# Padded Q/K projection weights in place of scatter DMAs, in a gated mix of infini-attention and a token-mixing MLP

## The chip, the cores and the metric

The kernel runs on one core of one Trainium2 chip. The metric is the device time of one execution in microseconds (us). An execution is called fast or slow by its time (slow is more than 1.5% above the fastest of the same kernel).

Engine names: PE is TensorE (matmul), PEld its weight loads, DVE VectorE, ACT ScalarE, POOL GpSimd, SP SyncE. L474 is line 474 of the kernel's file.

## The reference

The input x has 2048 rows of 640. One branch is attention with a compressive memory: 32 heads of 20 columns, four segments of 512 rows, causal softmax within a segment and a memory M, z carried from segment to segment. The other is an MLP that mixes along the rows. A gate mixes the two.

```python
g = sigmoid((x * gate_w).sum(-1, keepdims=True))
# branch a, for each segment s of 4:
p = softmax(qs @ ks.T * 20**-0.5 + causal_mask)
o = sig(beta) * (phi(qs) @ M) / (phi(qs) @ z + 1e-6) + (1 - sig(beta)) * (p @ vs)
M = M + phi(ks).T @ vs ;  z = z + phi(ks).sum(rows)
a = concat(o) @ wo
# branch b:
u = gelu(layernorm(x).T @ w1 + b1)      # 640 x 1536
b = (u @ w2 + b2).T                     # 2048 x 640
out = g * a + (1 - g) * b
```

## The kernel before

The 32 heads stand in eight groups of four. In the layout of a group (qA for Q, kA for K) each head has 32 of the 128 partitions: row 0 is a spare row (the "safe" variant puts the row maximum there; its partner in kA is -1), rows 1 to 20 are the head, the rest are zeros. The projection matmul makes 128 plain columns at a time, so 20-row heads lie across them, and small DMAs carry each head to its rows:

```python
def proj_T(s, which, dq):                   # dq = 0..4: 128 plain columns of wq or wk
    st = pl["stg"].tile([P, L], BF, ...)
    pq = p1([P, 512], name="pT" + which)
    for c in range(DC):                     # 5 matmuls of 512 columns
        nc.tensor.matmul(pq[:, 0:L], lhsT=w_sb[:, c, dq * P:(dq + 1) * P], rhs=xT[:, c, s * L:(s + 1) * L], ...)
    evac(st[:], pq[:, 0:L])
    for h in range(H):                      # every head that ends in these columns
        ...
        nc.sync.dma_start(out=dst[row:row + DH, g, :], in_=st[e0 - dq * P:e1 - dq * P, :])
```

The main loop runs over segments and groups. Beside a group's scores and exponentials it does the projections of the next segment (in groups 0 to 4 only), the previous group's product with V, and a part of the MLP's second half:

```python
for s in range(NSEG):
    for g in range(G):
        st_exp(s, g)                        # scores psB (32-row matmuls, one per head), exp on ScalarE, mask on GpSimd
        if prev is not None: pv_post(*prev) # pacc = P @ V, 21 columns for each head
        ...
        if g < TPS: nat_v(s + 1, g); nat_k(s + 1, g)
        ...
        if g < DC: proj_T(s + 1, "q", g); proj_T(s + 1, "k", g)
        if g % 2 == 0: tail_y(s * TPS + j)  # 24 matmuls of the MLP, result scaled into yb by ScalarE
        elif s >= 1:   tail_b(s - 1, j, ...) # output projection, store of one row tile through GpSimd
```

Ahead of it stands the prologue: transposes of x, segment 0's projections, layer-norm statistics, and the first MLP matmul (w1, six loads of 1 MB through three buffers).

## Time and profile before

| | before |
|---|---|
| time, median of the first 4 runs | 461.99 us (460.63 to 465.0) |
| span of the profiled run | 461.5 us, clock 0.86 |
| prologue, to the first exponential | 137.8 us |
| segments 0 to 3 | 81.3, 85.2, 78.1, 57.4 us |
| end, after the last exponential | 21.7 us |

The prediction below shows the table of stages. Two lines of the page give the whole at a glance: engine busy time, and the granted TensorE clock in 40 equal slices, in tenths of full speed.

```profile
PE 384.5 (83%) x3636; PEld 217.9 (47%) x3636; DVE 191.0 (41%) x469; ACT 251.7 (55%) x413; POOL 104.9 (23%) x174
...
PEclk9755989997997999956599998599989889877877
```

TensorE is busy 83% of the span, but the clock dips again and again below 9. The 30 clock records of this trace have only two values, 1.0 and 0.5; a 7 is a mixture. The profiled run took 463.31 us, 0.3% above the median.

```profile
L489 PE MATMUL pacc<-vs,PT 128*128 128x21 bf16 x116 | 4.6, 179 | 0.9 <-POOL PT L476 0.9
L471 PE MATMUL psB<-qA,kA 32*128 32x512 bf16 x12 | 2.6, 599 | 0.0
```

These are the groups without projections. TensorE looks 82 to 92% busy and yet gets a clock of 0.62 and 0.73. Its work there is in part scores of only 32 rows (32*128) and products of only 21 columns; the largest single group in the window, 24 full-height matmuls of the MLP, has 7.7 us.

### The profile page before, as it was taken

To read this page: it belongs to the slowest core of one execution; us is meant where nothing else is said; L and a number is where in the kernel's file an instruction comes from. 1 tells how busy PE (TensorE), PEld (TensorE's weight loads), DVE (VectorE), ACT (ScalarE), POOL (GpSimd) and SP (SyncE) were. 2 spreads that over 40 slices of the span, in tenths; PEclk is the share of its full clock that TensorE was granted. 3 is DMA by queue.
4 is the path that set the end of the run, shared out by engine and by line. 5 is a ranking of instruction groups with operands and counts; after the bars stand their busy time and mean duration, and the time that the engine had idled before them with its cause. 6 is when DMAs were issued, how large, how long until landed. Compare 5 with 4: busy or idle time off the path is not lost.

```text
span 461.5 us, 9298 instructions
## 1 busy us (share of the span) xinstructions
PE 384.5 (83%) x3636; PEld 217.9 (47%) x3636; DVE 191.0 (41%) x469; ACT 251.7 (55%) x413; POOL 104.9 (23%) x174
## 2 busy tenths in 40 slices
PE   3604969967989998878999998999979799999971
PEld 3501437744754555534355554445535445445451
DVE  7178145000003466540457585254645533332342
ACT  2933724210234768566566647575545778777810
POOL 3000000000012223124222322342323244433321
PEclk9755989997997999956599998599989889877877
DMA  7970011129003013102001310021131120000001
GB/s 257 330 201 0 23 25 25 25 51 243 1 19 124 20 27 93 25 19 70 3 22 38 91 38 24 20 84 26 40 89 39 26 78 22 16 16 15 3 31 48
DMA packets 27817, 27.06 MB, mean 59 GB/s; under 512 B 3700, under 2 KB 25716, under 8 KB 27764
## 3 DMA queue, kind: packets, MB, share of 16 engines
q1 hardware_dynamic: 25122, 17.45, 13.7%
q0 software_dynamic: 2432, 8.91, 5.9%
q8 instruction: 30, 0.49, 0.5%
q14 instruction: 23, 0.19, 0.1%
q10 hardware_dynamic: 210, 0.02, 0.0%
HBM read 18.50 MB, written 2.62 MB: 46 GB/s over the span
## 4 chain that ended last, share of the span: by engine, by line
PE 52%; ACT 12%; SPq 10%; DMA 9%; DVE 8%; issue 6%; POOL 2%; ACTq 0%; DVEq 0%; POOLq 0%
PE py L518 14%; PE psB L471 9%; ACT PT L474 8%; SPq L199 8%; PE pu L363 7%; PE pTq L189 4%; PE pTk L189 4%; PE pv L144 4%; PE pk L155 4%; DMA qA<-stg_q 3%; DMA wq_sb<-in_A_wq_dram 3%; PE pacc L489 3%; DVE stats L287 3%; PE po L546 2%; POOL PT L476 2%
## 5 line engine op out<-in xcount | busy, mean ns | idle before, releaser
L474 ACT ACTIVATE PT<-psB 128x1024 bf16<-128x1024 f32 (+3 forms) x256 | 167.2, 711 | 41.7 <-PE psB L471 35.4
L476 POOL TENSOR_SCALAR_AFFINE_SELECT PT<-PT 128x512 bf16<-128x512 bf16 x128 | 83.5, 653 | 174.4 <-ACT PT L474 171.8
L471 PE MATMUL psB<-qA,kA 32*128 32x256 bf16 (+3 forms) x512 | 75.2, 331 | 10.3 <-ACT PT L474 9.0
L518 PE MATMUL py<-uT,w2c 128*128 128x320 bf16 x384 | 76.4, 342 | 0.6 <-DVE aseg L432 0.6
L363 PE MATMUL pu<-xs,w1c 128*128 128x320 bf16 x384 | 54.1, 304 | 7.5 <-DMA w1c<-in_B_w_dram 7.5
L471 PEld LDWEIGHTS <-kA 32*128 32x128 bf16 x512 | 24.7, 92 | 67.5 <-issue 61.0
L518 PEld LDWEIGHTS <-w2c 128*128 128x128 bf16 x384 | 37.4, 106 | 25.0 <-issue 6.2
L363 PEld LDWEIGHTS <-w1c 128*128 128x128 bf16 x384 | 37.9, 99 | 23.1 <-DMA w1c<-in_B_w_dram 7.9
L489 PE MATMUL pacc<-vs,PT 128*128 128x21 bf16 x1280 | 44.9, 174 | 2.4 <-POOL PT L476 2.3
L489 PEld LDWEIGHTS <-PT 128*128 128x128 bf16 x1280 | 38.4, 97 | 15.5 <-issue 9.8
L508 POOL DMA_DIRECT2D w2c<-in_B_w_dram x8 | 8.5, 1062 | 149.7 <-PE pu L363 129.9
L522 ACT ACTIVATE yb<-py,omgb,omg 128x320 bf16<-128x320 f32 x32 | 18.0, 613 | 39.7 <-PE py L518 39.7
L395 DVE CAST vs<-pv 128x320 bf16<-128x320 f32 x24 | 10.9, 489 | 67.4 <-PE pv L144 67.4
L366 ACT ACTIVATE uT<-pu,b1t 128x320 bf16<-128x320 f32 x24 | 11.3, 523 | 49.6 <-PE pu L363 49.6
L144 PE MATMUL pv<-wv_sb,xT 128*128 128x320 bf16 x160 | 32.7, 310 | 5.1 <-ACT stg_q L343 3.0
L546 PE MATMUL po<-wo_sb,aT 128*128 128x320 bf16 x160 | 32.2, 327 | 2.2 <-DVE at L501 1.5
L189 PE MATMUL pTq<-xT,wq_sb 128*128 128x512 bf16 x100 | 30.8, 429 | 2.4 <-DVE phikb L135 1.8
L492 DVE RECIPROCAL rr<-pacc 128x16 f32<-128x16 f32 x32 | 8.2, 256 | 50.1 <-PE pacc L489 49.3
L189 PE MATMUL pTk<-xT,wk_sb 128*128 128x512 bf16 x100 | 28.5, 419 | 0.4 <-DVE phikb L135 0.4
L133 DVE TENSOR_SCALAR e_q<-qA 128x512 bf16<-128x512 bf16 x24 | 8.7, 363 | 41.0 <-DMA qA<-stg_q 40.9
L155 PE MATMUL pk<-wk_sb,xT 128*128 128x320 bf16 x120 | 24.4, 334 | 0.0
L395 DVE COPY aT<-pta 128x640 bf16<-128x640 bf16 x16 | 7.7, 488 | 39.5 <-PE pta L532 39.5
(103 smaller groups left out, 368.6 us busy)
## 6 DMA issues: line engine op xcount, KB each, us to landing
w1c<-in_B_w_dram SPq DMA_DIRECT2D x6, 1024.0 KB
w2c<-in_B_w_dram POOLq DMA_DIRECT2D x8, 768.0 KB, 5.7
xs<-in_A_x_dram SPq DMA_DIRECT2D x4, 640.0 KB
out_dram<-osb POOLq DMA_DIRECT2D x16, 160.0 KB, 2.2
kA<-stg_k SPq DMA_DIRECT2D x112, 20.0 KB
qA<-stg_q SPq DMA_DIRECT2D x112, 20.0 KB
wv_sb<-in_A_wv_dram SPq DMA_DIRECT2D x1, 800.0 KB
wk_sb<-in_A_wk_dram SPq DMA_DIRECT2D x1, 800.0 KB
```

Source lines behind the costliest of these rows:

```text
L144: nc.tensor.matmul(pv[hh][:, 0:HALF], lhsT=xT[:, c, t * P:(t + 1) * P], rhs=wv_sb[:, c, hh * HALF:(hh + 1) * HALF], start=(c == 0), stop=( ...
L155: nc.tensor.matmul(pk[hh][:, 0:HALF], lhsT=xT[:, c, t * P:(t + 1) * P], rhs=wk_sb[:, c, hh * HALF:(hh + 1) * HALF], start=(c == 0), stop=( ...
L189: nc.tensor.matmul(pq[:, 0:L], lhsT=w_sb[:, c, dq * P:(dq + 1) * P], rhs=xT[:, c, s * L:(s + 1) * L], start=(c == 0), stop=(c == DC - 1))
L199: nc.sync.dma_start(out=dst[row:row + DH, g, :], in_=st[e0 - dq * P:e1 - dq * P, :])
L363: nc.tensor.matmul(pu[hh][:, 0:HALF], lhsT=w1c[:, t, f2 * P:(f2 + 1) * P], rhs=hs[:, t, hh * HALF:(hh + 1) * HALF], start=(t == 0), stop=( ...
L395: nc.vector.tensor_copy(out=out_view, in_=ps_view)
L471: nc.tensor.matmul(psB[:, rr, 0:Nq], lhsT=kA[32 * r:32 * r + 32, g, jt * P:(jt + 1) * P], rhs=qA[32 * r:32 * r + 32, g, jt * P:L], start=T ...
L474: nc.scalar.activation(out=pt[:, hp * NRT:(hp + 1) * NRT, :], in_=psB[:, :, 0:Nq], func=ACT.Exp, scale=SCALE)
L476: nc.gpsimd.affine_select(out=pt[:, :, 0:P], in_=pt[:, :, 0:P], compare_op=ALU.is_ge, fill=0.0, base=0, pattern=[[0, HG], [1, P]], channel ...
L489: nc.tensor.matmul(pacc[:, it, r, :], lhsT=PT[jt][:, r, (it - jt) * P:(it - jt + 1) * P], rhs=vs[:, jt, HG * g + r, :], start=(jt == 0), s ...
L518: nc.tensor.matmul(py[hh][:, 0:HALF], lhsT=w2c[:, ft, (t % 2) * P:(t % 2 + 1) * P], rhs=uT[:, ft, hh * HALF:(hh + 1) * HALF], start=(ft == ...
L546: nc.tensor.matmul(po[hh][:, 0:HALF], lhsT=aT[:, c, :], rhs=wo_sb[:, c, hh * HALF:(hh + 1) * HALF], start=(c == 0), stop=(c == DC - 1))
```

## The change

The intent: place the 20 columns of each head at the right places of zero-padded weights wq_pad, wk_pad of 8 x 128 columns, once. Then the projection of a group comes out in the group's layout, and the 288 scatter DMAs go. The price is 8 instead of 5 projections for Q and for K in each segment, on an engine that is already the bound. The diff brings more than its title says: a new order of the prologue (MLP before the projections of segment 0), projections spread over all eight groups, yb on VectorE, stores and w2 loads on SyncE.

```diff
+    wq_pad = persist.tile([P, DC, G * P], BF, name="wq_pad")
+    wk_pad = persist.tile([P, DC, G * P], BF, name="wk_pad")
 ...
+        nc.gpsimd.memset(wq_pad[:], 0.0)
+        nc.vector.tensor_copy(out=wq_pad[:].rearrange("p c (h w) -> p c h w", w=32)[:, :, :, 1:1 + DH],
+                              in_=wq_st[:].rearrange("p c (h d) -> p c h d", d=DH))
 ... (wk_pad likewise)
-    for i in range(2):
-        nc.vector.memset(qAb[i][:], 0.0)
-        nc.vector.memset(kAb[i][:], 0.0)
-        def proj_T(s, which, dq): ...            # with its scatters
+        def pg_q(s, g):
+            pq = p1([P, 512], name="pq")
+            for c in range(DC):
+                nc.tensor.matmul(pq[:, 0:L], lhsT=wq_pad[:, c, g * P:(g + 1) * P], rhs=xT[:, c, s * L:(s + 1) * L], ...)
+            evac(d["qA"][:, g, :], pq[:, 0:L])
+            ... (phi of it)
+        def pg_k(s, g): ...                      # likewise, kbias adds the -1 of the spare row
 ... (in the loop)
-                    if g < DC:
-                        proj_T(s + 1, "q", g)
-                        proj_T(s + 1, "k", g)
+                    pg_q(s + 1, g)
+                    pg_k(s + 1, g)
 ... (yb)
-                nc.scalar.activation(out=yb[...], in_=py[hh][:, 0:HALF], func=ACT.Identity, scale=omg[...], bias=omgb2[...])
+                if fast: nc.vector.tensor_scalar(out=yb[...], in0=py[hh][:, 0:HALF], scalar1=omg[...], scalar2=omgb2[...], ...)
 ... (queues)
-            nc.gpsimd.dma_start(out=w2c[:], ...)
+            nc.sync.dma_start(out=w2c[:], ...)
-            nc.gpsimd.dma_start(out=out[0, t * P:(t + 1) * P, :], in_=osb[:])
+            nc.sync.dma_start(out=out[0, t * P:(t + 1) * P, :], in_=osb[:])
 ... (prologue: statistics in two halves, MLP, transposes and gate, then segment 0's projections)
```

## The prediction

> **What bounds the kernel now.** I first read the list of cores: one core, 461.5 us, mean granted clock 0.86. Then I cut the span at the events that separate its stages (first projection matmul, first MLP matmul, last MLP matmul, first exp of each of the four attention segments, last exp) and asked for busy time per stage.
>
> ```profile
> core 0: us, PE busy (x) PEld busy (x) DVE busy (x) ACT busy (x) POOL busy (x), PEclk, DMA share, GB/s
> 0.00:41.40 41.40, 12.55 (x165) 10.71 (x166) 25.41 (x71) 18.87 (x29) 4.22 (x22) 0.72 0.73 219
> 41.40:74.90 33.50, 28.35 (x174) 16.00 (x173) 15.75 (x40) 19.67 (x31) 0.00 (x0) 0.89 0.09 20
> 74.90:134.80 59.90, 52.38 (x375) 36.94 (x373) 1.38 (x3) 10.39 (x22) 0.00 (x0) 0.94 0.26 64
> ...
> 137.80:219.10 81.30, 73.64 (x713) 37.79 (x713) 37.86 (x90) 53.00 (x90) 22.60 (x34) 0.83 0.19 55
> 219.10:304.30 85.20, 80.25 (x793) 43.15 (x792) 47.34 (x112) 52.72 (x89) 24.53 (x38) 0.86 0.14 41
> 304.30:382.40 78.10, 70.54 (x728) 37.59 (x726) 38.01 (x94) 48.91 (x80) 25.99 (x39) 0.93 0.16 47
> 382.40:439.80 57.40, 55.40 (x611) 28.59 (x610) 18.13 (x44) 45.92 (x72) 22.12 (x37) 0.85 0.04 13
> 439.80:461.50 21.70, 9.66 (x79) 6.18 (x78) 7.13 (x16) 0.01 (x1) 3.21 (x6) 0.69 0.11 42
> ```
>
> Prologue: 137.8 us to the first exp, of which the first 41.4 have almost no TensorE work. The first three segments (244.6 us) are TensorE-bound: it is busy 90 to 94%, at a clock of 0.83 to 0.93. The last has ScalarE at 80%. The groups of instructions give the unit costs.
>
> ```profile
> L474 ACT ACTIVATE PT<-psB 128x1024 bf16<-128x1024 f32 (+3 forms) x256 | 167.2, 711 | 41.7 <-PE psB L471 35.4
> L522 ACT ACTIVATE yb<-py,omgb,omg 128x320 bf16<-128x320 f32 x32 | 18.0, 613 | 39.7 <-PE py L518 39.7
> L189 PE MATMUL pTq<-xT,wq_sb 128*128 128x512 bf16 x100 | 30.8, 429 | 2.4 <-DVE phikb L135 1.8
> L189 PE MATMUL pTk<-xT,wk_sb 128*128 128x512 bf16 x100 | 28.5, 419 | 0.4 <-DVE phikb L135 0.4
> ```
>
> One group of four heads needs 8 exps, 8 x 711 ns = 5.7 us of ScalarE. The scatters show in the list of waits, beside the one stall of the MLP:
>
> ```profile
> DVE e_q L133 <- DMA qA<-stg_q: 40.9, 15, 6.2
> ACT yb L522 <- PE py L518: 39.7, 15, 6.3
> PE pu L363 <- DMA w1c<-in_B_w_dram: 7.5, 1, 7.5
> ```
>
> The 40.9 us are VectorE's, not the bound's; in the chain of waits that DMA has only 3% of the span (some 15 us). The 7.5 us are TensorE's: the w1 loads share SyncE's queue with the segment-0 scatters. In time order, this is how an even head group of segment 1 starts:
>
> ```profile
> 233.06 1.13 ACT L522 ACTIVATE yb<-py,omgb,omg 128x320 bf16<-128x320 f32 x2 [5.74 <-PE py L518]
> 233.37 0.40 PE L471 MATMUL psB<-qA,kA 32*128 32x512 bf16 x4
> ...
> 234.08 3.82 ACT L474 ACTIVATE PT<-psB 128x1024 bf16<-128x1024 f32 x5
> ```
>
> ScalarE stands idle 5.7 us while TensorE does projection and MLP work, then does yb, and only then the exps, whose input came during yb. And the prologue waits for the layernorm statistics, through the three transposes of the fast/safe test:
>
> ```profile
> 40.46 0.17 DVE L308 TENSOR_REDUCE gstat<-x 128x1 f32<-128x16 f32 x1
> 40.78 0.80 PE L318 MATMUL pg<-ident_f,gstat 128*1 128x128 f32 x3 [20.22 <-DVE gstat L308]
> 41.37 2.34 PE L189 MATMUL pTq<-xT,wq_sb 128*128 128x512 bf16 x5
> ```
>
> [...] at 47.63 and 48.71 us two groups of five 512-column projections start 1.08 us apart, 216 ns each[...]. [...] in 192.5 to 219.1 us, the light end of segment 0, TensorE is busy 21.8 of 26.6 us and the granted clock is 0.62. [...] The scatters go through SyncE[...]: they stand in the chain in pieces of 1.9 to 2.5 us, and issuing one costs SyncE 0.71. [...] no row of before is like the new padding copy.
>
> **The change, part by part.**
>
> *Projections.* 5 chunks of 128 columns become 8 padded groups: 3 more groups x 2 (q, k) x 5 matmuls = 30 more per segment, 30 x 0.216 = 6.5 us at full clock. The three segments that project ahead take +19.4; segment 0's also +6.5. Evictions: 16 instead of 10 per segment at 0.69 us on VectorE, +4.1 us, beside other work. Where the old loop projected only in head groups 0 to 4 and left 5 to 7 nearly empty, the new order has pq and pk in all eight; in groups 4 to 7 they lie between score matmuls, in ScalarE-limited time.
>
> *Scatters.* 288 small DMAs (144 each for q and k) go, with the waits of phi(q) on them and the block of w1 (7.5 us).
>
> *yb moves to VectorE* (in the diff, not in its title). In the last segment ScalarE sets the pace: from 376.15 to 388.87 us, two head groups, 12.72 us, it has 2 x 5.67 + 1.13 = 12.47 us of work. So 4 x 1.13 = 4.5 us go there; in segments 0 to 2 a little less than 0.6 us for each of 12 (exp input ready at about 233.6, exp at 234.1), some 6 us.
>
> *Prologue.* New order: statistics, MLP, transposes, gate, then segment-0 projections.
> - Statistics start with the first quarter of x, at 5.3 us, not at 26 (there behind 9 us of memsets and the gate). One row tile costs 0.86 us (28.18 to 29.04), 16 cost 13.8; with pieces between them 20.4. Then two padding copies stand before the last steps[...], then 1.9 us of small instructions: gstat at about 26, pg, first MLP matmul at 26.7.
> - 384 MLP matmuls at 136 ns = 52.4 (52.38 busy measured)[...]: 82.
> - 80 transposes evicted by two engines, 6 us; 80 gate matmuls 2.7; branch: 92.
> - V and K rows: 80 x 0.136 = 10.9, but VectorE needs 2.7 us per tile and four PSUM buffers recycle through ScalarE: 14. Memory update 2. Q and K 80 x 0.216 = 17.3. First exp at 126 to 127, against 137.8: **-11 us**. The statistics save 15, the stall 7.5; transposes and gate, no longer under the loads, give back 9[...].
>
> *Main loop.* [...] a head group lasts the exp-paced stretch (about 5.8 us before, 5.5 without yb) plus what the new order puts after the last score matmul. Counting matmuls there, in segment 1 before: 5.3, 3.9, 5.9, 5.0, 5.9, 0, 1.8, 0, sum 27.8; with 8 x 5.8 this makes 74.2 at full clock against 85.2 measured, a factor of 1.15. Segment 0 gives 71.9 against 81.3 (1.13), segment 2 66.4 against 78.1 (1.18). After, the same count gives 72.0, 78.8 and 72.8. With a factor of 1.10 (no DMA waits, fewer light stretches) they take 79.2, 86.7 and 80.1, together 246 against 244.6. The last segment: 57.4 - 4.5 = 52.9. Main loop 299 against 302: **-3**.
>
> *End.* Stores on SyncE instead of GpSimd, 0.55 us each of GpSimd time gone: -1 of 21.7.
>
> Sum: 461.5 - 11 - 3 - 1 = 446.5; I say 446.
>
> **The rivals.**
> 1. *The extra matmuls are paid in full.* If the factor stays at 1.15, the three segments take 257, +12.6 on 244.6: total about 457, the same within 2%. For it: TensorE already at 90 to 94%. Against: a part lies in exp-paced time.
> 2. *The evened load keeps the clock up.* The lost time of before is mostly in the light head groups (0.62, 0.73 and 0.84 at the ends of segments 0 to 2). If pq and pk hold the clock near 1 there, the factor falls to 1.04: 232.5, total about 432.
> 3. *VectorE becomes the bound.* It takes yb (some 0.49 us each) and the added evictions: segment 1 from 47.3 to about 55 us of 87. Not in sum[...]; bursts in head group 4 could add 1 us to each group: about 460.
> 4. *Prologue.* [...]
>
> **Range and chances.** Rivals 2 and 1 give 432 to 457; 4 us more for the prologue on the slow side, and 2 on the other: 430 to 461. The 2% line is at 452.7; my middle is 6.7 below it, and about two thirds of my range: faster 0.67, same 0.27, slower 0.06 (it would need rivals 1, 3 and 4 together).
>
> **What would show it.** First MLP matmul near 27 us, ending near 82, without a wait for w1; first exp near 127; segments near 79, 87, 80 and 53 us; ScalarE above 85% busy in the last; no scatter DMAs; granted clock in head groups 5 to 7 above 0.85. Wrong if the first MLP matmul comes after 33, if a segment exceeds 90 us, or if py or pq wait for VectorE by more than 10 us in all.

Three terms of its sums went: the time of the two padding copies ahead of gstat, a slow-clock term at the start of the MLP, and what rival 4 put on the prologue. With the cut terms the forecast came to 26.7 us for the first MLP matmul, 82 for the end of the MLP, -11 us for the prologue and 446.5 us in all; the terms that are left would give 23 and 75.4 us for the first two, and -13.5 us. The 216 ns are the distance between starts (109 of 122 such gaps at full clock in before are 215 or 216 ns); the 419 ns of the row are the mean length of a record, and these records overlap. The 2.7 us per tile on VectorE match three pairs of rows in the trace of before (0.95, 0.89 and 0.89 us). The 6 us for the evictions of the transposes are the author's estimate.

## More of the kernel before

The following answers are the busy times in groups 5 to 7 of segments 0 and 1 (columns: window and length, then PE, PEld, DVE, ACT, POOL busy with instruction counts, clock, DMA share, GB/s).

```profile
192.50:219.10 26.60, 21.82 (x212) 9.82 (x209) 6.68 (x21) 17.94 (x30) 8.51 (x13) 0.62 0.15 42
279.10:304.30 25.20, 23.12 (x240) 11.49 (x236) 10.75 (x29) 17.96 (x30) 8.98 (x14) 0.73 0.16 49
```

## The result

The kernel after takes 419.31 us (median of 10 runs, 418.39 to 420.61) against 461.99 (15 runs, 455.97 to 466.68). A ratio here is the mean time of one kernel's fast runs over the mean of the other's fast runs of the same rounds, with the profiled runs left out and "fast" judged among the rest, so it is not quite the ratio of the medians; it is 0.912, with a 95% interval of 0.909 to 0.915. The prediction of 446 (430 to 461) had the direction, but the result is 27 us below it and outside the range.

The answering two lines of the page of after:

```profile
PE 374.4 (90%) x3756; PEld 219.0 (53%) x3756; DVE 235.0 (56%) x542; ACT 226.4 (54%) x364; POOL 106.7 (26%) x162
...
PEclk9999999989999999998799999999999999999988
```

There are 120 more matmuls and 10 us less busy time. The clock is at 9 or more almost everywhere. The stages of after, cut at the same kinds of events (first MLP matmul, last MLP matmul, first exponential of each segment, last exponential; columns as above):

```profile
24.20:78.80 54.60, 54.60 (x389) 38.62 (x388) 1.93 (x10) 18.86 (x32) 0.00 (x0) 1.00 0.47 130
78.80:120.60 41.80, 38.88 (x358) 24.04 (x356) 30.53 (x57) 10.67 (x23) 8.21 (x4) 0.96 0.01 1
120.60:193.20 72.60, 70.54 (x724) 38.12 (x722) 46.54 (x100) 48.61 (x80) 23.42 (x33) 1.00 0.08 23
193.20:277.50 84.30, 81.36 (x839) 45.54 (x838) 56.95 (x129) 49.03 (x80) 21.61 (x34) 0.96 0.09 26
277.50:350.90 73.40, 71.08 (x762) 39.09 (x761) 49.02 (x109) 45.27 (x72) 20.91 (x33) 1.00 0.11 32
350.90:400.70 49.80, 48.45 (x627) 27.36 (x625) 23.98 (x56) 40.73 (x64) 19.83 (x31) 1.00 0.04 15
400.70:417.10 16.40, 8.92 (x78) 5.89 (x75) 7.14 (x16) 0.00 (x0) 0.64 (x1) 0.81 0.17 57
```

| stage | before | predicted | after | gain |
|---|---|---|---|---|
| prologue | 137.8 | 126.5 | 120.6 | 17.2 |
| segment 0 | 81.3 | 79.2 | 72.6 | 8.7 |
| segment 1 | 85.2 | 86.7 | 84.3 | 0.9 |
| segment 2 | 78.1 | 80.1 | 73.4 | 4.7 |
| segment 3 | 57.4 | 52.9 | 49.8 | 7.6 |
| end | 21.7 | 20.7 | 16.4 | 5.3 |
| sum | 461.5 | 446.1 | 417.1 | 44.4 |

The segments 0 to 2, which got 19.4 us more matmul work, became 14.3 us shorter. What the clock takes can be read from a table of stages: a stage of length t at mean clock c loses about (1 - c) t of TensorE time. Before, that is 0.17 x 81.3 + 0.14 x 85.2 + 0.07 x 78.1 = 31.2 us in segments 0 to 2, after it is 0.04 x 84.3 = 3.4 us. So 27.8 us come back, more than the padding costs. This is bookkeeping, as it counts idle time at half clock too. What the two tables show directly is that TensorE's idle time in these segments fell from 20.2 to 7.3 us, and its busy time by 1.45 us in spite of the added matmuls.

How the prologue starts in after, in order of time (start, us, engine, line, operation, bracket: what ended the idle time before it):

```profile
19.97 1.12 DVE L233 COPY wq_pad<-wq_st 128x3200 bf16<-128x3200 bf16 x1
...
23.50 0.17 DVE L191 TENSOR_REDUCE gstat<-x 128x1 f32<-128x16 f32 x1
...
23.81 0.58 PE L197 MATMUL pg<-ident_f,gstat 128*1 128x128 f32 x2 [17.04 <-DVE cmask L268]
```

The statistics are there at 23.50 us, against 40.46 before. The padding copy takes 1.12 us, less than the cut term of the prediction allowed.

The end, before and after (same columns):

```profile
454.64 1.01 DVE L550 SCALAR_TENSOR_TENSOR osb<-po,gt,yb 128x320 bf16<-128x320 f32 x2 [2.79 <-DMA out_dram<-osb]
455.95 0.54 POOL L553 DMA_DIRECT2D out_dram<-osb  x1 [3.26 <-DVE osb L550]
```

```profile
412.26 1.01 DVE L521 SCALAR_TENSOR_TENSOR osb<-po,gt,yb 128x320 bf16<-128x320 f32 x2 [0.52 <-PE po L517]
```

Before, the last output tile waits 2.79 us for an earlier store to give its buffer back, and 5.9 us lie between the end of that tile's work (455.65) and the end of the span (461.5). After, there is no such wait, and 3.8 us lie between (413.27 and 417.1).

### The profile page after: what moved, and what is told of

Read it like the earlier page. It is cut to its first block, busy times and chain, and to the rows that moved or that the text cites. A ratio compares the mean times of both kernels' runs of the same rounds, so it can differ in the third digit from the quotient of the medians.

```text
span 417.1 us, 9052 instructions
## 1 busy us (share of the span) xinstructions
PE 374.4 (90%) x3756; PEld 219.0 (53%) x3756; DVE 235.0 (56%) x542; ACT 226.4 (54%) x364; POOL 106.7 (26%) x162
## 3 DMA queue, kind: packets, MB, share of 16 engines
q1 hardware_dynamic: 31842, 21.11, 17.2%
## 4 chain that ended last, share of the span: by engine, by line
PE 79%; ACT 9%; DVE 4%; DMA 3%; SPq 2%; issue 2%; POOL 0%; ACTq 0%; POOLq 0%; DVEq 0%
PE psB L437 13%; PE py L484 13%; PE pu L222 13%; PE pq L367 9%; PE pk L394 9%; ACT PT L440 7%; PE pv L328 6%; PE po L517 5%; PE pk L339 4%; PE pacc L455 3%; DMA wk_sb<-in_A_wk_dram 2%; SPq L140 2%; PE pta L503 1%; ACT xT L246 1%; DMA xs<-in_A_x_dram 1%
## 5 line engine op out<-in xcount | busy, mean ns | idle before, releaser
L437 PE MATMUL psB<-qA,kA 32*128 32x256 bf16 (+3 forms) x512 | 68.4, 305 | 7.5 <-ACT PT L440 7.5
L484 PE MATMUL py<-uT,w2c 128*128 128x320 bf16 x384 | 60.1, 300 | 0.0
L437 PEld LDWEIGHTS <-kA 32*128 32x128 bf16 x512 | 24.5, 91 | 60.9 <-issue 54.9
L222 PE MATMUL pu<-hs,w1c 128*128 128x320 bf16 x384 | 54.6, 306 | 0.0
L394 PE MATMUL pk<-xT,wk_pad 128*128 128x512 bf16 x160 | 45.0, 381 | 0.0
L367 PE MATMUL pq<-xT,wq_pad 128*128 128x512 bf16 x160 | 44.6, 381 | 0.0
L484 PEld LDWEIGHTS <-w2c 128*128 128x128 bf16 x384 | 35.2, 98 | 15.8 <-issue 1.2
L489 DVE TENSOR_SCALAR yb<-py,omg,omgb 128x320 bf16<-128x320 f32 x32 | 18.1, 606 | 24.8 <-PE py L484 24.8
L397 DVE TENSOR_SCALAR kA<-pk,kbias 128x512 bf16<-128x512 f32 x32 | 24.0, 748 | 12.3 <-PE pk L394 10.2
L318 DVE CAST qA<-pq 128x512 bf16<-128x512 f32 x32 | 22.0, 688 | 11.5 <-PE pq L367 11.5
L517 PE MATMUL po<-wo_sb,aT 128*128 128x320 bf16 x160 | 27.9, 310 | 0.5 <-DVE aT L318 0.5
L313 ACT ACTIVATE e_q<-e_q 128x512 bf16<-128x512 bf16 x24 | 15.0, 626 | 20.6 <-DVE e_q L312 20.6
```

The source lines that it names most:

```text
L222: nc.tensor.matmul(pu[hh][:, 0:HALF], lhsT=w1c[:, t, f2 * P:(f2 + 1) * P], rhs=hs[:, t, hh * HALF:(hh + 1) * HALF], start=(t == 0), stop=( ...
L367: nc.tensor.matmul(pq[:, 0:L], lhsT=wq_pad[:, c, g * P:(g + 1) * P], rhs=xT[:, c, s * L:(s + 1) * L], start=(c == 0), stop=(c == DC - 1))
L394: nc.tensor.matmul(pk2[:, 0:L], lhsT=wk_pad[:, c, g * P:(g + 1) * P], rhs=xT[:, c, s * L:(s + 1) * L], start=(c == 0), stop=(c == DC - 1))
L397: nc.vector.tensor_scalar(out=d["kA"][:, g, :], in0=pk2[:, 0:L], scalar1=kbias[:, 0:1], scalar2=None, op0=ALU.add)
L437: nc.tensor.matmul(psB[:, rr, 0:Nq], lhsT=kA[32 * r:32 * r + 32, g, jt * P:(jt + 1) * P], rhs=qA[32 * r:32 * r + 32, g, jt * P:L], start=T ...
L484: nc.tensor.matmul(py[hh][:, 0:HALF], lhsT=w2c[:, ft, (t % 2) * P:(t % 2 + 1) * P], rhs=uT[:, ft, hh * HALF:(hh + 1) * HALF], start=(ft == ...
```

## The experiments

Twelve kernels were run; all gave correct results. Each batch of four shared one chip and its runs of before (medians 461.46, 460.40 and 462.62 us). Ratios of different batches that are less than about 1% apart are not told apart here. First comes the theory, then the runs by question. The theory after reading the traces was: the padding pays because it evens TensorE's load, and the clock follows the load. The main rivals were that yb on VectorE, the vanished scatter waits, the queues or the new prologue order did it.

**The padding alone (b_pad).** The kernel before with padded weights, one projection of Q and K in each of the eight groups and no scatters. The zeroing of qA and kA falls away with the scatters. Order of the prologue, yb and queues stay.

```diff
-        nc.vector.memset(qAb[i][:], 0.0)
-        nc.vector.memset(kAb[i][:], 0.0)
+    nc.vector.tensor_copy(out=w_pad[...][:, :, :, 1:1 + DH], in_=w_sb[...])      # for q and k
-                    if g < DC: proj_T(s + 1, "q", g); proj_T(s + 1, "k", g)      # 128 plain columns, then scatters
+                    proj_T(s + 1, "q", g); phi_q(s + 1, g); proj_T(s + 1, "k", g) # w_pad, straight into qA, kA
```

> The kernel before with the padded projections alone: padded weights built by two VectorE copies, eight groups spread over eight head groups, no scatters; the order of the prologue, the statistics, yb on ScalarE and the stores stay as before. Theory of the clock: segments 0 to 2 at a clock above 0.95 and 225 to 235 us together (244.6 before), prologue within 2 us of before (6.5 us more matmuls, 7.5 us less stall), total 443 to 452 us. Rival (most of the gain is the new prologue order and yb on VectorE): 456 to 465 us, clock below 0.92.

Measured: 424.56 us (421.56 to 427.75), ratio 0.9225 (0.912 to 0.933). That is most of the gain, and more than I expected (443 to 452 us): segments 0 to 2 came out as forecast, the prologue did not. The MLP and segment 3 of its stages, and the moment of the statistics:

```profile
61.60:115.20 53.60, 53.49 (x415) 38.39 (x411) 3.48 (x7) 12.67 (x26) 0.00 (x0) 1.00 0.22 60
...
346.10:402.30 56.20, 54.04 (x622) 28.75 (x619) 19.07 (x48) 45.68 (x72) 21.95 (x36) 0.88 0.04 13
```

```profile
30.57 0.17 DVE L304 TENSOR_REDUCE gstat<-x 128x1 f32<-128x16 f32 x1
```

The first exponential comes at 118.1 us, 19.7 earlier than before and even 2.5 earlier than in after, in the old order of the prologue. Two things go with it. VectorE no longer zeroes qA and kA (four memsets of 1.76 us), and its statistics begin at 5.28 us, no longer behind that and the gate; they are there at 30.57 instead of 40.46, and the first MLP matmul comes at 61.6 instead of 72.3. What the zeroing alone is worth and what the changed order of VectorE's work was not separated. And the MLP runs its 53.6 us without the stall for w1 (62.6 before), because no scatters stand in SyncE's queue ahead of the w1 loads. Segments 0 to 2 take 73.2, 81.0 and 73.8 us, all at clock 1.00. Segment 3 and the end (21.4 us) stay as before.

**yb on VectorE alone (b_yb_dve), and taken back from after (a_yb_act).** The edit of the first is the yb part of the diff above; the second is its reverse.

> The kernel before with yb on VectorE and nothing else changed. My prediction: 4.5 us off the last segment and some 6 off the others: 449 to 454 us, clock of segments 0 to 2 still 0.83 to 0.93. Rival (yb between the exps is what makes the light stretches and so the low clock): clock above 0.95, time below 440.

Measured: 461.31 us (452.81 to 464.21); three of four runs were slow, so there is no ratio. The one fast run, 452.81 us, lies within the expected 449 to 454, the median does not: this run decides nothing. The last segment of its profile (a slow run) takes 55.7 us.

> The kernel after with the scaling of the MLP output back on ScalarE in every segment. Theory: worth little in segments 0 to 2 where TensorE sets the pace (each within 1.5 us of after), but in the last segment, where the exponentials on ScalarE set the pace, it puts the eight 600 ns evictions back: last segment 55 to 58 us instead of 49.8 and a clock of 0.85 to 0.95 there; in all 424 to 428 us, 1.0% to 2.2% slower than after. Rival (ScalarE never binds; the last segment is shorter after for another reason, such as the stores): 418 to 421 us with the last segment at 49 to 51.

Measured: 421.58 us (419.29 to 421.84), ratio 0.919, which is 0.8% above the ratio of after, from another batch. The last segment takes 50.2 us at clock 1.00 with all eight evictions back on ScalarE. So yb was not what shortened segment 3. My expectation of 55 to 58 us was wrong, and so was the prediction's 4.5 us.

**Is it the load that keeps the clock? (b_fill)** To the kernel before I added ten useless matmuls of 512 columns and 128 rows in each of groups 5 to 7 of segments 0 to 2. That is 90 x 0.216 = 19.4 us of TensorE time that computes nothing used.

```diff
+                    else:                                   # groups 5 to 7
+                        pd = p1([P, 512], name="pfill")
+                        for c in range(2 * DC):
+                            nc.tensor.matmul(pd[:, 0:L], lhsT=wo_sb[:, c % DC, 0:P], rhs=xT[:, c % DC, 0:L], ...)
```

> The kernel before, plus ten 512-column matmuls of useless work in each of head groups 5 to 7 of segments 0 to 2 (90 matmuls, 19.4 us of TensorE at full clock; nothing reads them). Theory (the light head groups let the clock fall to half, and the change's main gain is that it fills them): the granted clock over the three segments rises from 0.87 to above 0.95 and the time stays within 2% of before or falls, 445 to 465 us, although there is more work. Rival (matmuls are paid in full, and the lower clock only goes along with waits for the scatters): clock unchanged near 0.87, time up by 15 to 22 us, to 477 to 484.

Measured: 461.93 us (457.43 to 464.27), ratio 1.0009 (0.991 to 1.011). The added 19.4 us cost nothing: the clock of the fast runs rose from 0.86-0.88 to 0.90-0.92 and paid for them. Groups 5 to 7 of segment 0, to be read beside the window of 26.60 us above:

```profile
195.20:218.70 23.50, 22.46 (x232) 10.67 (x228) 6.97 (x21) 17.56 (x29) 8.65 (x13) 0.93 0.15 46
```

With 6.5 us more work, this stretch is 3 us shorter, at a clock of 0.93 instead of 0.62. It is the best of the three: in segment 1 it takes 24.5 us instead of 25.2 (clock 1.00 instead of 0.73), in segment 2 27.9 instead of 21.1 (0.81 instead of 0.84). Together they take 75.9 us instead of 72.9.

**What the clock goes with.** I then took the clock records and all matmuls of the traces apart. All changes of the clock in these traces lie on a grid of 3.413 us (in before, every record but the last, which the end of the trace cuts off, lasts 3.413 us or a multiple of it, from 1 to 16 times). For each window of that grid I summed the columns of its matmuls, once plainly and once weighted by the share of the 128 rows in use, and divided by 8192 columns, or 16 matmuls of 512 columns, about what a window holds at full clock (at the measured 0.216 us from start to start it is 15.8 of them). Scores count a quarter in the second sum, as they use 32 of 128 rows. They mostly run two at a time: in before 202 of 233 clusters are pairs that start 3 to 6 ns apart, and in 25 all four heads start within 10 ns. The finished analysis covers 14 traces, all full-clock windows after the first 60 us:

| weighted use of the window | windows | followed by half clock |
|---|---|---|
| below 0.30 | 61 | 61 |
| 0.30 to 0.40 | 66 | 30 |
| 0.40 and more | 1204 | 0 |

Of these, before alone has 8 of 8, 6 of 9 and 0 of 70; after alone has 4 of 4, no window in the middle row, and 0 of 95.

Plain column use separates far worse: of the windows with 0.5 to 0.7 of it, 28 of 155 are followed by half clock. In the light groups of before TensorE does mostly scores and 21-column products (164 of the 212 matmuls in the window of 26.60 us above) with pauses between (idle 4.8 us); the five windows in these groups or at their edge that were followed by half clock have 0.18 to 0.33. At half clock the highest weighted use of a window is 0.51 in before and in after (512-column matmuls then start 0.427 us apart instead of 0.216). The way back has about the same line: the clock returned after all 61 half-clock windows with 0.40 or more, after 23 of 49 with 0.35 to 0.40 and after none of 73 below (in before alone 8 of 8, 5 of 10 and 0 of 12). So a light stretch can stay slow for several windows: in before for five, 17.07 us from 195.49 us on.

In all these traces but one, a window with few rows at work is mostly also one in which matmuls stream for a small part of the time (concurrent scores counted once). To tell "how long TensorE is busy" from "how many rows are at work", one run more was needed; it is the one that makes the difference.

**The same useless work on 32 rows (b_fill32).**

```diff
-    nc.tensor.matmul(pd[:, 0:L], lhsT=wo_sb[:, c % DC, 0:P], rhs=xT[:, c % DC, 0:L], ...)
+    nc.tensor.matmul(pd[:, 0:L], lhsT=wo_sb[0:32, c % DC, 0:P], rhs=xT[0:32, c % DC, 0:L], ...)
```

> The kernel before with the same ten useless 512-column matmuls in head groups 5 to 7 of segments 0 to 2 as in the run with 128 rows, but each over 32 rows only: the same TensorE time, a quarter of the rows at work. Theory: what the clock goes by is matmul columns weighted by the share of the 128 rows in use (in the traces so far every 3.41 us window followed by half clock had at most 0.38 of it, plain column use didn't separate them). Then the filler lifts the weighted use of a light head group by only about 0.05 to 0.1 and the clock of segments 0 to 2 stays at 0.85 to 0.93, while 19 us more TensorE work has to be paid at that clock: 470 to 485 us, 2% to 5% slower than before. Rival (any busy TensorE time counts): as with 128 rows, clock 0.95 to 1.0 in segments 1 and 2 and 458 to 466 us. A second rival (it is the useless work's effect on waits and order, not the clock): also 458 to 466 us.

Measured: 476.02 us (469.72 to 478.68), ratio 1.042 (1.033 to 1.051). Of the three runs in this ratio two are listed as slow beside the faster profiled run; the one left gives 1.035. The profiled run was fast. The same window, and the useless matmuls in it:

```profile
189.40:216.90 27.50, 25.82 (x231) 12.45 (x227) 7.16 (x21) 17.53 (x29) 8.70 (x13) 0.68 0.14 40
```

```profile
L589 PE MATMUL pfill<-xT,wo_sb 32*128 32x512 bf16 x30 | 11.7, 507 | 0.0
```

TensorE is busy 25.8 of 27.5 us and the clock is 0.68. At full clock these matmuls start about 0.22 us apart in its trace, as the 128-row ones do, so they take the same time (30 of them are 11.7 us busy here at a mean clock of 0.68, the 30 of 128 rows 10.5 us at 0.93); seven windows in which matmuls had streamed for 0.50 to 0.82 of the window (concurrent scores counted once), but whose weighted use was 0.23 to 0.33, were followed by half clock. Groups 5 to 7 of the three segments together take 87.7 us, against 75.9 with the 128-row filler. Both rivals expected 458 to 466 us and fell: in these two runs the clock went with the rows at work (0.93 with 128, 0.68 with 32), not with the busy time. Whether the chip counts rows or something that goes with them can't be told from these runs.

**The projections of after packed into groups 0 to 3 (a_packed).** All work and layouts of after, but two groups' projections in each of the first four groups and none in the last four.

```diff
-                    pg_q(s + 1, g); pg_k(s + 1, g)
+                    if g < 4:
+                        for gg in (2 * g, 2 * g + 1): pg_q(s + 1, gg); pg_k(s + 1, gg)
```

> The kernel after, with the sixteen projections of the next segment packed into head groups 0 to 3 (two groups each) instead of one in each of the eight. Same matmuls, no scatters, yb on VectorE. Theory of the clock: groups 4 to 7 are light again, the granted clock of segments 0 to 2 falls below 0.92 and the time rises to 432 to 450 us; about 15 us of that come at full clock already, because the packed matmuls stand after the last score matmul instead of between score matmuls. Rival (the even spread doesn't matter, only the scatters had to go): clock stays at 0.97 or more, time within 4 us of 419.

Measured: 430.45 us (424.64 to 433.84, two of four runs slow), ratio 0.938 (0.929 to 0.947), so 2.9% above the ratio of after with the same instructions; the only run in it that is listed as fast, 428.98 us, gives 0.933, 2.3% above. Segment 0 of its profile (a fast run), then groups 5 to 7 of segments 0 and 1:

```profile
120.50:200.60 80.10, 74.36 (x751) 40.43 (x749) 47.42 (x105) 49.33 (x80) 23.62 (x33) 0.95 0.07 21
...
180.00:200.60 20.60, 18.89 (x219) 9.05 (x215) 4.80 (x13) 15.91 (x24) 7.89 (x13) 0.79 0.14 40
265.00:283.30 18.30, 17.77 (x237) 9.85 (x233) 9.22 (x22) 15.27 (x24) 7.07 (x12) 1.00 0.19 56
```

Segment 0 takes 80.1 us instead of 72.6, while segment 1 is 1.6 us shorter. Each side of my expectation was half wrong: the time is above the rival's 415 to 423 us and just short of the theory's 432, but the clock of segments 0 to 2 came to 0.97, as the rival had it, not below 0.92. In segment 0 the light groups lose the clock. In segment 1 they have 1.00 without any projections, where before has 0.73 in 25.2 us. So in this segment lumps did not cost the clock; before also has the late phi of scattered heads and yb on ScalarE in these groups, and which of that matters was not separated. In the profiles segments 0 to 2 take 244.6 us in before, 236.1 here and 230.3 in after: 8.5 of the 14.3 us come without the even spread, and the spread is worth 5.8. By the bookkeeping used above some 3 us of these are clock (0.05 x 80.1 + 0.03 x 82.7 = 6.5 us lost, against 3.4 in after); the rest was not taken apart.

**The w1 stall alone (b_w1q).** Before, with the fourth to sixth w1 loads on GpSimd's queue.

```diff
-            nc.sync.dma_start(out=w1c[:], in_=w1v[...])
+            eng = nc.sync if fp < 3 else nc.gpsimd
+            eng.dma_start(out=w1c[:], in_=w1v[...])
```

> The kernel before with nothing changed but the queue of the later w1 loads (the fourth to sixth), which GpSimd issues instead of SyncE, so that they don't stand behind the scatters of segment 0. Theory: the 7.5 us stall of the MLP is caused by that order alone; then the MLP lasts 53 to 56 us instead of 62.6, the first exponential comes at 128 to 132 us instead of 137.8 and the time is 452 to 456 us. Rival: the loads come no sooner because the scatters' own transfers or the buffers hold them: MLP still 60 us or more, 458 to 463 us.

Measured: 449.02 us (448.73 to 451.64), ratio 0.983 (0.974 to 0.992), better than expected. The MLP's group of matmuls, whose 7.5 us wait for w1 is gone:

```profile
L364 PE MATMUL pu<-xs,w1c 128*128 128x320 bf16 x384 | 52.5, 299 | 0.0
```

The MLP takes 53.5 us instead of 62.6 and the first exponential comes at 129.4, which is 8.4 us earlier. So the queue order alone made the stall. The rest of the difference to the profiled before lies in the segments at a somewhat higher clock (0.88 and 0.89 in segments 0 and 1, against 0.83 and 0.86), which is within what runs of before scatter among themselves.

**The stores and w2 loads (b_sp, a_st_pool).** The first moves them to SyncE in before, the second moves them back to GpSimd in after; both edits are the queue lines of the diff above.

> The kernel before with only the output stores and the loads of the second MLP weights on SyncE. Theory: the end falls from 21.7 to 16 to 18 us as it rose from 16.4 to 22.2 when after got the GpSimd queue back, and the rest stays: 454 to 458 us. Rival: on SyncE the loads and stores stand behind the scatters of the segment ahead, which waits more in segments 1 and 2 (py waits for w2c): 459 to 466 us.

Measured: 450.22 us (447.42 to 452.18), ratio 0.986 (0.976 to 0.995). The end takes 18.1 us instead of 21.7. The larger part is segment 3:

```profile
378.00:427.60 49.60, 48.06 (x611) 27.05 (x610) 19.07 (x44) 44.80 (x72) 20.27 (x32) 1.00 0.04 14
```

It takes 49.6 us at clock 1.00 instead of 57.4 at 0.85, with yb still on ScalarE. I had expected the rest to stay as it was.

> The kernel after with the output stores and the loads of the second MLP weights issued by GpSimd again, as in before. Theory: the 5 us that the end became shorter (from the last exponential to the end, 21.7 before, 16.4 after) come from this; then the end is 20 to 22 us and the time 422.5 to 425.5 us, 0.8% to 1.5% slower than after. Rival: the end is shorter because the clock and the backlog of output tiles are better, and the queue is worth nothing: end 16 to 17.5, time 418 to 421 us.

Measured: 428.03 us (421.26 to 431.52; two of four slow), ratio 0.925 from the fast runs, 1.5% above that of after. The end takes 22.3 us in its profile, as expected. That profile is of a slow run, so its last segment (59.7 us at 0.80) is not evidence by itself. Fast profiles agree, however: with stores on GpSimd the last segment took 56.2 (b_fill), 52.3 (b_fill32), 56.2 (b_pad) and 55.7 us (b_w1q), with stores on SyncE 49.2 to 50.2 in all seven (after, a_packed, a_yb_act, b_sp, and the three runs below). Why is only argued: before, four stores of 0.56 us stand between masks on GpSimd in that segment (at 394.68 and 408.87 for example; no w2 load is issued there), may delay the products with V a little, and the four windows of segment 3 that were followed by half clock had a weighted use of 0.298 to 0.358, in the middle row of the table above or just below it.

**Everything but the new prologue (b_pad_yb_sp).** The edits of b_pad, b_yb_dve and b_sp together in the kernel before.

> The kernel before with padded projections and no scatters (its prologue order kept: transposes, statistics and segment-0 projections before the MLP), and besides with yb on VectorE and the stores and second-weight loads on SyncE. Theory: what separated the run with padding alone (424.6) from after (419.3) is the end and the last segment, not the new order of the prologue; then the end is 16 to 17.5 us instead of 21.3, the last segment 50 to 53 at a clock near 1, and the time 415 to 420 us, as fast as after or faster. Rival: the new order of the prologue is worth the 5 us: 421 to 425 us.

Measured: 413.04 us (412.24 to 419.23), ratio 0.902 (0.892 to 0.911), a little faster than after (0.912). Its segments 1 and 3:

```profile
190.30:271.70 81.40, 78.43 (x839) 44.79 (x838) 56.91 (x129) 49.04 (x80) 21.04 (x33) 1.00 0.09 27
...
345.10:394.80 49.70, 48.36 (x625) 27.24 (x622) 23.95 (x56) 40.70 (x64) 19.82 (x31) 1.00 0.04 15
```

The new order of the prologue thus earned nothing (with some small changes that after brings along, such as Tanh for the gate). It costs 2.5 us to the first exponential. Another 2.9 us of the difference of the profiles lie in segment 1 (81.4 here, 84.3 in after), where after has two half-clock windows at its start. Why they are there was not tested: four other kernels made from after have 0.96 or 0.97 in segment 1, a fifth (a_st_pool) has 1.00.

**A version that beats both (a_early_late, a_v2).** In after, TensorE does next to nothing until 23.8 us and then has 80 transposes and the gate to do behind the MLP (78.7 to 85.7). a_early_late does these first and moves the flag's test (which picks the fast or the safe variant) behind the MLP.

```diff
+        for t0 in range(0, ST, 4): ...transposes of x, evicted by ScalarE...     # ahead of the statistics
+        gl = ...; gate matmuls
-        ...the same behind the MLP
-        pg, gred, flag_f, flag_i, flag_dram      # ahead of the MLP
+        pg, gred, flag_f, flag_i, flag_dram      # behind it
```

> A candidate to beat both: the kernel after with the 20 transposes of x and the gate's matmuls moved ahead of the MLP, into the time in which TensorE waits for the layer-norm statistics, and the test of the flag moved behind the MLP. Theory: what the MLP now leaves behind it (78.7 to 85.7 in after, 7 us) leaves the chain, while the first MLP matmul stays at 24 to 25 us as the statistics decide it; first exponential at 112 to 115 us instead of 120.6, time 410 to 414 us (1.2% to 2.2% faster than after). Rival: the work of evicting the transposes on ScalarE delays the normalised x by as much, or the flag's test now adds 2 to 4 us behind the MLP: first exponential 118 to 122, time 417 to 422 us.

Measured: 417.35 us (416.89 to 421.79), ratio 0.914: no gain, as the rival had it. The first MLP matmul came at 26.3 instead of 24.2 us, because ScalarE squared wq for the flag (2.85 us) before it normalised x. Behind the MLP the flag's test held the projections back from 80.7 to 84.9 us. a_v2 mends both: the squares write into the buffer of x, so they have to wait until x has been normalised, and the test lies within the MLP.

```diff
+            if fp == 1: ...gstat; squares of wq and wk, out=xs[:, ST - DC:ST, :]; padding copies...
+            if fp == 3: ...pg, gred, flag_f, flag_i, flag_dram...
```

> The candidate of the last batch (417.3 us) mended where its profile showed what the rearranged prologue lost: the squares of the weights for the flag's test now come on ScalarE after the normalised x, not before (they held it up by 2.85 us), and the three transposes and the small instructions of the flag's test lie inside the MLP, not behind it (80.7 to 84.9 us). Theory: first MLP matmul at 23.5 to 24.5 us instead of 26.3, segment-0 projections start within 1 us of the MLP's end, first exponential at 112 to 114 us, time 409 to 413 us. Rival: the branch and the flag's round trip through memory, or the clock, hold the projections up anyway: first exponential 116 to 119, time 414 to 418 us.

Measured: 410.57 us (408.89 to 411.01), ratio 0.897 (0.892 to 0.902), 1.6% below the ratio of after and the lowest median here (its interval overlaps that of b_pad_yb_sp). The first MLP matmul, at 24.9 us, came a little later than expected. The start and the end of its MLP:

```profile
24.93 2.32 PE L208 MATMUL pu<-hs,w1c 128*128 128x320 bf16 x8 [3.55 <-ACT hs L191]
...
80.54 1.52 PE L327 MATMUL pv<-wv_sb,xT 128*128 128x320 bf16 x10 [0.96 <-ACT uT L211]
```

The projections follow the MLP after 0.96 us, and the first exponential comes at 113.2.

The steps in one table, from the profiled runs. Columns: what is switched on, first exponential, segments 0 to 2 together, segment 3, end.

| | first exp | 0 to 2 | 3 | end | span |
|---|---|---|---|---|---|
| before | 137.8 | 244.6 | 57.4 | 21.7 | 461.5 |
| + padding, no scatters (b_pad) | 118.1 | 228.0 | 56.2 | 21.4 | 423.7 |
| + yb, SyncE stores (b_pad_yb_sp) | 118.1 | 227.0 | 49.7 | 16.7 | 411.5 |
| + new prologue order (after) | 120.6 | 230.3 | 49.8 | 16.4 | 417.1 |
| prologue mended (a_v2) | 113.2 | 230.2 | 49.7 | 15.4 | 408.5 |

## Why the prediction was wrong

**The step that failed is the one that reads "With a factor of 1.10 (no DMA waits, fewer light stretches) they take 79.2, 86.7 and 80.1".** The count under it was right: 72.0, 78.8 and 72.8 us at full clock, and with the clock at 1.00 in all three segments b_pad_yb_sp measured 72.2, 81.4 and 73.4, a factor of 1.015; after itself has 1.03. The error there is 246.0 - 230.3 = 15.7 us of the 29.0 by which the stages were off (446.1 against 417.1). Rival 2 had the clock right, and its size as well: it gave 232.5 us for the three segments, and 230.3 was measured. I took the middle between two rivals, and no line that I had read spoke for the middle. That segment 1 came close (86.7 predicted, 84.3 measured) is luck: it has two half-clock windows that b_pad_yb_sp, with 81.4 us, has not.

**The reason that I gave for the factor was too vague.** I had seen that the light groups lose the clock (0.62) while TensorE is busy 82%, and did not ask why. The rows at work go with it: the useless work on 128 rows lifted the clock of the first such stretch from 0.62 to 0.93, the same on 32 rows only to 0.68. The pq and pk of the padded layout have 128 rows and 512 columns, and they came to lie in exactly the groups that lacked such work. The light end of segment 0 was predicted at a clock above 0.85; groups 5 to 7 of after have 1.00. a_packed shows that this is not all: without projections in these groups it loses the clock in segment 0 alone. How much of the clock comes from the vanished waits for scatters stays open.

**Rival 1 fell** (the extra matmuls paid in full, about 457), **and so did rival 3**: VectorE went up to 57 us in segment 1, and yet TensorE's waits for it after the first matmul come to about 5 us in the whole span.

**The prologue: predicted -11, measured -17.2.** The times after the change were close: first MLP matmul 24.2 (26.7 predicted), end 78.8 (82), first exponential 120.6 (126 to 127). The terms that were mis-sized are the padding copies (1.1 us each in the trace, less than the cut term allowed, so rival 4 fell too) and transposes with gate (7.0 instead of 9). Wrong was what I credited. The text has the new order saving 15 us in the statistics. The old order with padding is 2.5 us better, since its 10 us in the statistics come with the padding itself, which needs no zeroing on VectorE (b_pad). The 7.5 us of the w1 stall were right (8.4 with b_w1q).

**The padding copies and two readings.** No row of before was like these copies, and my size for them rested on nothing in the traces. In after they take 1.12 and 1.11 us for 3200 elements a partition each, although the padded side is written in runs of 20. Two readings were incomplete. The pieces of 1.9 to 2.5 us of the scatters leave out one of 5.29 us in the same list (at 334.64 us). And the 216 ns were read from two groups of matmuls; they stand by the whole trace of before, where most projection matmuls in a stream start 215 to 216 ns apart.

**Segment 3: predicted -4.5 by yb, measured -7.6, by another cause.** "4 x 1.13 = 4.5 us go there" is refuted by a_yb_act (50.2 us with yb on ScalarE). Moving the stores and w2 loads did it (b_sp: 49.6 us), together with the clock, which went from 0.85 to 1.00. The pace that I read from two head groups of ScalarE was not what the segment as a whole followed: half of that stretch (376.15 to 388.87) lies ahead of segment 3, which begins at 382.4, and all of it is at full clock, while the segment's drops come from 396.9 on.

**The end: predicted -1, measured -5.3.** I counted 0.55 us of issuing time per store. The runs show two other costs: the last store of the span lands about 2 us later from GpSimd, and an output tile waits 2.8 us for its buffer. The times from issue to landing do not show it: their median over the 16 stores is 1.9 us in after (SyncE) and 2.2 in before (GpSimd), but for the five stores in the windows of the end it is 2.6 and 2.3, the other way. What shows the gain is the length of the end itself, 18.1 against 21.7 us in b_sp.

Right were the vanished scatters, the absence of a w1 wait, and that py and pq hardly wait for VectorE. My sign "ScalarE above 85% busy in the last segment" was wrong: it is 40.73 of 49.8 us, 82%.

## What to carry to other kernels

Where TensorE is the bound, read the granted clock by stage before counting instructions (in before it was 0.83 to 0.93 in segments 0 to 2, in after 0.96 to 1.00). In the traces none of the 1204 windows of 3.413 us with a weighted use of 0.40 or more was followed by half clock, and all 61 below 0.30 were; other kernels were not tested. Here more work was faster than less, as waits went with it and the clock stayed up (segments 0 to 2 of b_pad: 19.4 us more matmul work, 228.0 instead of 244.6 us, at 1.00); spread evenly it was faster still (230.3 us in after against 236.1 in a_packed). A high busy share did not mean a full clock: in b_fill32 TensorE was busy 25.8 of 27.5 us, much of it with 32 of 128 rows, at a clock of 0.68. And when a change has several parts, switch them on one by one: here the part with the largest diff, the reordered prologue, earned nothing, while two lines about queues were worth some 6 us (1.4% in before, 1.5% in after, by the ratios).
